# A linear-attention stage worked on pairs of chunks, two tokens to a partition, ahead of a convolution stage

## The chip, the cores and the metric

One core of a Trainium2 chip runs the whole kernel. The metric is device time in microseconds. Three runs of the kernel before took 157.04, 157.25 and 161.11 us, the median is 157.25. One further run was taken with the profiler; its time was 157.08 us, and the span that its trace covers is 155.3 us.

## What is computed

Two stages follow each other. The first is a linear attention with a decaying state: for each of 4 batches and 8 heads, 768 tokens, head size 48. The second is a gated circular convolution over the 768 tokens, in 384 channels (8 heads x 48), done with Fourier transforms. The reference, cut to what matters:

```python
for t in range(S):                                   # stage one, B=4, H=8, S=768, D=48
    cur = einsum('bhd,bhe->bhde', u[None] * kt, vt)
    y[:, :, t] = einsum('bhd,bhde->bhe', rt, state + cur)
    state = wt[:, :, :, None] * state + einsum('bhd,bhe->bhde', kt, vt)
x = y.transpose(0, 2, 1, 3).reshape(B, S, H * D)
proj = x @ w_proj                                    # stage two: three blocks of 384 columns
x1, x2, x3 = split(proj, 3)
x2_conv = irfft(rfft(x2, axis=1) * rfft(filter_fft, axis=0)[None], axis=1)
out = (x1 * x2_conv * x3) @ w_out
```

w lies between 0.8 and 0.95. All inputs and the output are float32.

## The kernel before

**Stage one, by chunks of 128 tokens.** 24 chunks (6 a batch) are worked one after the other. A chunk's 128 tokens lie in the 128 partitions. Loads go by groups: the first two groups hold one chunk each, all others two (`group`, line 1425). Each of w, k, r and v is loaded a chunk at a time, with runs of 48 numbers (192 bytes) in DRAM (line 1438); for the groups in `CASTS` v is loaded by POOL's queue instead and cast to bf16 on the way (line 1435). For each chunk i (`first`, line 1465):

- `ln`: ACT takes the log of w (line 1444); `cs`: PE sums the logs over the tokens with two triangular masks (lines 1473 and 1474, 384 columns each) and over the whole chunk with four matmuls of one column (line 1476); `ex`: ACT takes the exponential (line 1482); `kq`: DVE multiplies k and r by it (`scale`, shown at line 1328); `ph`: the chunk's whole decay (line 1493).
- `tr` and `qk`: k and q are turned by eight PE transposes (line 1501) and copied out of PSUM (line 1332 on ACT, 1334 on DVE); for the last chunks a DMA transpose on SP's queue does this instead (line 1507).
- `sc`: the scores of the 8 heads, eight matmuls of 48 x 128 x 128, two heads at a time in the upper and the lower half of the rows (line 1519). `mt` and `mc`: the mask, either as a product on DVE (line 1535) or as a copy on ACT and a cut on POOL by `affine_select` (line 1540).
- `kv`, `ki`, `su`: the state's update, eight matmuls of 64 columns (line 1560), the old state added with an identity (line 1566), and the decay on DVE (line 1570).
- `yi`, `ys`, `y`: the output y gathers in PSUM the term with u (`vc`, made by `rk`, `ru`, `rh`, `cc`, `vc` on POOL and DVE, added at line 1580, or later by DVE at line 1609), the term from the state (line 1589) and the masked scores times v (line 1597). `xn`, `yt`, `xT`: y is copied as bf16, turned (PE at line 1621, or DMA transpose at line 1630) and stored as xT.

**Stage two** (`second`, line 1761) for a batch: projections of xT (`p`, `q` at line 1768 and `xw` at line 1809), a sum and a difference of the two halves (`sd`, line 1820), the forward transform as matmuls with a table F (line 1655), products with the filter's spectrum (`u`, `p`, lines 1843 and 1846), the inverse transform (`E`, line 1865, with adds `aE` at 1903 and 1908 and `dE` at 1918), the gate (`yE`), the output projection (`o`, line 1950) and the store (line 1966). The tables F and mi are sines, made by ACT (line 1672) from angles that DVE and POOL compute; this needs another function table on ACT (`trig`, line 1666, and `table`, line 1716, back again).

**The order of the work** is written out by hand as the string `ORDER`: each line names an operation, the engine that does it ("-" for not at all), and, for what PE writes, the PSUM bank. Each engine works off its part in that order. `wproj`, `wout` and the casting loads of v stand in POOL's part, all other DMAs in SP's. A third word on POOL's lines ties it behind a named DVE instruction (line 1218). `warm n b` (line 1376) issues matmuls of zeros (line 1380) that no result needs. Stage two of a batch is interleaved with stage one of the next.

Of the kernel before, what the change touches and what calls it, by code (L numbers as in the profile page):

```python
# [20 lines left out]
L = 128  # L21
# [15 lines left out]
ADD, DVE2, ACT2, POOL2, FOLD, WIDE = "V", "M", "N", "C", "Q", "X"  # L37

NLW, NLD, NG, NF, NS, NX, NO = 3, 4, 3, 4, 3, 3, 4
CASTS = (2,4,6,8,10,12,)  # L40
NV, NVL = 6, 3
NTURN = 8
# [6 lines left out]
warm 16 4  # L49
first A  # L50
imaps G
smalls D
zeros D
pads D
signs D
lw0 S
lw3 S
kz1 D
ln0 A
maske G  # L60
lw2 S
lr0 S
u S
maskn G smalls
maps G
ang2 D
ia0.0 G
ia1.0 G
maski G
kz0 G pads  # L70
ang1 D
ang0 D
ia2.0 D
cs0 P 2
lk0 S
ln2 A
ex0 A
ew0 -
kq0 D
warm 8 0  # L80
warm 6 1
cs3 P 0
ex3 -
ia2.1 D
kw0 -
lw1 S
ur A
warm 4 5
um P 6
warm 5 5  # L90
tr0 P 4
lk3 S
lr3 S
ew3 X
lr1 S
lk1 S
kz2 G
ph0 A
ub A
ln1 A  # L100
lv0 S
rk0 G ang0
kz3 G kq0
ru0 G
rh0 D
cc0 D
qk0 A
kq3 -
kw3 G rh0
lv2 G cc0  # L110
warm 3 5
cs1 P 5
warm 3 7
sc0 P 3
mt0.1 D
mc0.1 -
lr2 S
lk2 S
vb0 G
vc0 G rh0  # L120
ex1 A
ph3 A
mt0.0 D
ew1 -
lv3 G
warm 3 7
cs2 P 0
warm 4 7
tr3 P 4
ex2 A  # L130
kq1 D
qk3 A
kw1 -
warm 2 7
tr1 P 7
mc0.0 -
rk1 D
ru1 D
rh1 G rk1
qk1 D  # L140
ph1 A
warm 3 2
sc3 P 4
kv0 P 2
su0 D
ew2 -
kq2 D
kw2 -
lv1 S
warm 2 3  # L150
sc1 P 6
yi0 P 2
y0 P
mt1.1 D
lw4 S
mt3.1 -
xn0 A
xa0 -
mt3.0 N
ph2 A  # L160
rk2 D
ru2 D
rh2 G rk2
vb1 A
tr2 P 3
warm 3 2
ki1 P 5
warm 2 2
kv1 P
lw5 S  # L170
lk4 S
lr4 S
qk2 A
ln3 A
mt1.0 D
cc1 D
yt0 P 2
lr5 S
lk5 S
lv5 S  # L180
warm 3 4
sc2 P 0
su1 D
warm 1 3
ki2 P 5
kv2 P
cc2 D
su2 D
cs4 P 6
ex4 A  # L190
wproj1 G
mc3.1 -
ki3 P 4
kv3 P
mt2.1 A
mc1.1 -
ia0.1 G
vc1 D
xT0 D
warm 2 3  # L200
yi1 P 2
ys1 P
vc2 G
mt2.0 D
mc1.0 -
y1 P
ew4 -
su3 D
mc2.1 G mt1.0
kq4 D  # L210
mc2.0 -
cs5 P 0
xn1 A
ex5 A
warm 1 4
yi2 P 3
ys2 P
y2 P
kw4 -
kq5 D  # L220
ew5 -
lw7 S
ph4 A
xn2 A
tr4 P 6
xa1 -
xa2 -
kw5 -
qk4 D
yt1 P 3  # L230
tr5 P 2
yi3 P 6
qk5 D
yt2 P 4
ph5 A
wproj0 G kq4
mc3.0 C
lv4 S
xT2 D
ys3 P  # L240
lr7 S
y3 P
xn3 D
sc4 P 4
mt4.0 D
xa3 -
trig A
sin2 A
rk3 G qk4
ru3 G qk5  # L250
warm 1 0
yt3 P 7
xT1 D
mt4.1 A
ia1.1 G mt4.0
warm 3 0
sc5 P 5
mt5.1 -
lw6 S
mt5.0 M  # L260
xw0.0 P 0
rh3 D
cc3 D
vb3 G rh3
sin1 A
vc3 G mt5.0
ki4 P 2
cxw0.0 D
xT3 A
warm 1 3  # L270
xw0.2 P 6
sin0 A
kv4 P
is A
cxw0.2 D
su4 D
warm 5 4
p0.2.0 P 5
p0.0.0 P 0
table A  # L280
lr6 S
lk6 S
lk7 S
mc4.1 G
filt S
lw8 S
lw9 S
cp0.0.0 D
yi4 P 6
yi5 P 2  # L290
ys5 P
lv7 G cxw0.2
mc5.0 -
mc5.1 -
ys4 P
y5 P
lk9 S
lk8 S
mc4.0 -
y4 P  # L300
xn4 D
if1 A
ln4 A
xn5 A
lv8 S
cs6 P 0
xa5 -
yt5 P 3
if0 A
ex6 A  # L310
lr9 S
xa4 -
yt4 P 2
xT5 D
xT4 D
cs7 P 6
ew6 -
kq6 D
ex7 A
ew7 -  # L320
xw0.4 P 2
lr8 S
kq7 D
ph6 A
cxw0.4 A
sd0.1.0 D
kw7 -
sd0.0.0 D
rk4 G
p0.2.1 P 4  # L330
cp0.2.1 A
ph7 A
kw6 -
lw10 S
p0.0.1 P 0
tr7 P 3
qk7 D
fsd0 D
fsd1 D
tr6 P 7  # L340
ru4 D
cp0.0.1 A
qk6 A
cp0.2.0 A
lv9 S
f0.2 P 0
cf0.2 A
sc6 P 6
mt6.1 -
mc6.1 -  # L350
mt6.0 N
f0.0 P 4
sc7 P 2
cf0.0 A
warm 2 0
h1 P 0
ln5 A
lv6 G sd0.1.0
h2 P 6
rh4 G fsd1  # L360
mt7.1 -
mt7.0 M
mc7.0 -
hc1 A
mc7.1 -
cc4 D
h0 P 2
hc2 A
kv6 P 4
hg1 D  # L370
hg2 D
hc0 A
cs8 P 0
su6 D
mc6.0 C
vc4 G
warm 2 5
yi6 P 6
y6 P
ex8 A  # L380
ew8 -
hg0 D
xn6 A
yi7 P 4
ys7 P
y7 P
xn7 A
xa7 -
xa6 -
cs9 P 6  # L390
kq8 D
yt6 P 3
ki7 P 2
kv7 P
su7 D
wproj2 G
yt7 P 4
xT7 D
ex9 A
xT6 A  # L400
kq9 D
kw8 -
rk5 G
ph8 A
ru5 D
rh5 D
cc5 D
ew9 -
tr8 P 5
ki8 P 2  # L410
qk8 A
ph9 A
vb5 G xT7
vc5 G
xw1.0 P 0
cxw1.0 A
kw9 -
tr9 P 3
qk9 A
kv8 P  # L420
sc8 P 4
su8 D
mt8.1 -
lw11 S
f0.1 P 0
ki9 P 6
kv9 P
mt8.0 M
if2 A
lk10 S  # L430
lk13 S
mc8.0 -
cf0.1 A
sc9 P 2
su9 D
q0.2.1 P 7
lr10 S
mt9.0 N
lk11 S
lr11 S  # L440
mt9.1 -
mc9.1 -
q0.0.1 P 5
lr13 S
yi9 P 0
q0.2.0 P 4
yi8 P 2
xq0.0.1 -
u10.0 D
lw12 S  # L450
ys9 P
ln6 A
ys8 P
cq0.0.1 D
lw13 S
mc8.1 -
y8 P
lv11 G su9
mc9.0 C
warm 5 2 192  # L460
y9 P
cs10 P 5
lr12 S
lv12 S
xq0.2.1 -
u00.0 D
xq0.2.0 -
xn8 A
xn9 A
q0.0.0 P 2  # L470
cq0.2.0 D
cq0.2.1 D
xq0.0.0 -
xa8 -
lk12 S
lv10 G
rk6 G
cq0.0.0 D
xa9 -
gq0.0.0 -  # L480
yt9 P 4
ex10 A
xT9 A
ru6 D
kq10 D
yt8 P 7
xT8 A
cs11 P 0
ex11 A
if3 A  # L490
kq11 D
warm 1 4
xw1.2 P 2
ew10 -
kw10 -
lk15 S
lv13 S
rh6 G ru6
cc6 D
ph10 A  # L500
lr15 S
gq0.2.0 -
lw15 S
lr14 S
p1.2.0 P 4
tr10 P 7
p1.0.0 P 5
cxw1.2 A
qk10 A
ew11 -  # L510
kw11 -
ph11 A
cp1.2.0 A
cp1.0.0 A
tr11 P 2
q1.0.0 P 0
# [1532 lines left out]
```

## Time and profile before

| | |
|---|---|
| profiled execution | 157.08 us, span 155.3 us |
| median of the runs shown | 157.25 us |
| PE, DVE, ACT, POOL busy | 142.3, 135.5, 117.5, 102.0 us |
| DMA packets, of them under 512 bytes | 112534, 108545 |
| moved | 27.12 MB, 175 GB/s over the span |
| share of the chain by engine | PE 65%, DVE 11%, DMA 9%, ACT 4%, SP's queue 4% |

How to read it: the span runs from the first to the last instruction of the profiled execution. A matmul's end is modelled, and matmuls overlap, so the price of one in a row of many is the distance of their starts. PE is the engine's matmuls, PEld its weight loads. In the rows of groups stand the line, the engine, the operation, out<-in, the count, then busy time in us and the mean of one in ns, then the idle time ahead of it and who ended it. Rows of stages give start:end, length, then busy time and count of each engine, the granted TensorE clock, the DMA share and GB/s. Rows of the chain give start, duration and the work. The line of DMA digits has 40 slices of 3.9 us.

### The profile page before, as it was taken

How to read it: one execution, taken by the hardware profiler on the slowest of the kernel's cores; microseconds unless marked ns; L12 is line 12 of the kernel's file. 1: busy time of each engine (PE TensorE's matmuls, PEld its weight loads, DVE VectorE, ACT ScalarE, POOL GpSimd, SP SyncE). 2: the span in 40 equal slices, each digit the busy share in tenths (PEclk: the TensorE clock that was granted, in tenths of full speed). 3: DMA queues.
4: the chain of work that ended last, by engine and by line, in shares of the span. 5: the costliest groups of instructions: out<-in, count | busy, mean ns of one | idle time of the engine just before them, and what ended most of it. 6: DMA issues, size and time to landing. Idle time of an engine off the chain costs nothing.

```text
span 155.3 us, 4220 instructions
## 1 busy us (share of the span) xinstructions
PE 142.3 (92%) x1634; PEld 89.4 (58%) x1634; DVE 135.5 (87%) x258; ACT 117.5 (76%) x195; POOL 102.0 (66%) x106
## 2 busy tenths in 40 slices
PE   7999894999999999999799999999999997999860
PEld 2455554656646767666566676665666664666430
DVE  4849984696999998999999999999999988799950
ACT  4584774897899894999879989989965575667650
POOL 6679595968229479589957988678796650802600
PEclk9999999699999999999999999999999999999997
DMA  5999999979999999899999918999997535000784
GB/s 105 227 212 218 194 145 215 200 135 339 177 187 213 198 181 180 142 199 176 187 192 201 179 25 144 220 193 189 178 183 149 155 122 209 0 0 34 294 330 159
DMA packets 112534, 27.12 MB, mean 175 GB/s; under 512 B 108545, under 2 KB 111106, under 8 KB 112514
## 3 DMA queue, kind: packets, MB, share of 16 engines
q1 hardware_dynamic: 98434, 24.49, 73.9%
q0 software_dynamic: 14080, 2.36, 20.0%
q8 instruction: 13, 0.21, 0.6%
q14 instruction: 7, 0.06, 0.1%
HBM read 22.41 MB, written 4.72 MB: 175 GB/s over the span
## 4 chain that ended last, share of the span: by engine, by line
PE 65%; DVE 11%; DMA 9%; ACT 4%; SPq 4%; issue 2%; DVEq 0%; ACTq 0%
PE banks L1768 13%; PE banks L1655 10%; PE banks L1380 7%; PE banks L1809 6%; PE banks L1950 5%; DMA kr<-in_k_dram 4%; PE banks L1865 4%; PE banks L1501 4%; SPq L1438 4%; PE banks L1519 4%; PE banks L1597 3%; DMA w<-in_w_dram 3%; DMA xT<-xn 3%; PE banks L1589 2%; PE banks L1473 2%
## 5 line engine op out<-in xcount | busy, mean ns | idle before, releaser
L1768 PE MATMUL banks<-xT,wproj 128*128 128x384 bf16 x144 | 27.3, 326 | 1.1 <-DVE xT L1334 1.0
L1328 DVE TENSOR_TENSOR kq<-banks,kr 128x768 bf16<-128x768 f32 x23 | 21.6, 950 | 3.1 <-DMA kr<-in_k_dram 2.7
L1328 POOL TENSOR_TENSOR vc<-vb,cc 128x768 bf16<-128x768 bf16 (+1 forms) x12 | 18.7, 1562 | 6.0 <-DVE sd L1820 3.1
L1328 POOL TENSOR_TENSOR rk<-kr 128x768 bf16<-128x768 f32 (+1 forms) x11 | 19.5, 1773 | 4.1 <-DMA kr<-in_k_dram 2.1
L1332 ACT ACTIVATE x<-banks 128x768 bf16<-128x768 f32 (+1 forms) x26 | 17.5, 687 | 5.2 <-PE banks L1809 3.0
L1482 ACT ACTIVATE banks<-banks 128x768 f32<-128x768 f32 x23 | 18.2, 798 | 1.9 <-PE banks L1476 1.6
L1535 DVE TENSOR_TENSOR mt<-banks,mask_excl 128x512 bf16<-128x512 f32 (+1 forms) x24 | 18.1, 772 | 1.3 <-PE banks L1519 1.1
L1768 PEld LDWEIGHTS <-wproj 128*128 128x128 bf16 x144 | 13.5, 98 | 9.3 <-issue 1.2
L1380 PE MATMUL banks<-wt 128*128 128x512 bf16 (+1 forms) x56 | 16.9, 397 | 1.1 <-DVE scl L1394 1.1
L1809 PE MATMUL banks<-wproj,xT 128*128 128x384 bf16 x72 | 13.7, 326 | 1.5 <-DMA xT<-xn 1.0
L1435 POOL DMA_DIRECT2D vb<-in_v_dram x12 | 11.3, 938 | 4.6 <-DVE sd L1820 3.3
L1540 POOL TENSOR_SCALAR_AFFINE_SELECT mt<-mt 128x512 bf16<-128x512 bf16 (+1 forms) x14 | 11.6, 834 | 3.5 <-ACT mt L1332 3.5
L1950 PE MATMUL banks<-wout,y 128*128 128x384 bf16 x72 | 13.3, 326 | 0.7 <-DVE y L1328 0.4
L1655 PE MATMUL banks<-sd,F 128*128 128x384 bf16 (+1 forms) x96 | 13.7, 328 | 0.0
L1501 PE MATMUL banks<-ident,kq 128*128 128x128 bf16 x144 | 11.1, 222 | 2.6 <-DVE kq L1328 2.1
L1332 ACT ACTIVATE qk<-banks 128x1024 bf16<-128x1024 bf16 x12 | 12.3, 1023 | 1.1 <-PE banks L1501 0.9
L1444 ACT ACTIVATE lg<-w 128x768 bf16<-128x768 f32 (+1 forms) x13 | 10.4, 798 | 3.2 <-DMA w<-in_w_dram 3.1
L1455 POOL TENSOR_TENSOR rk<-rk 128x384 bf16<-128x384 bf16 (+1 forms) x8 | 7.4, 921 | 7.7 <-DVE rk L1328 7.6
L1332 ACT ACTIVATE X<-banks 128x768 bf16<-128x768 f32 x12 | 9.8, 815 | 3.0 <-PE banks L1655 2.9
L1501 PEld LDWEIGHTS <-kq 128*128 128x128 bf16 x144 | 9.0, 98 | 4.9 <-DVE kq L1328 2.9
L1655 PEld LDWEIGHTS <-F 128*128 128x128 bf16 (+1 forms) x120 | 8.4, 103 | 5.6 <-issue 1.0
L1328 DVE TENSOR_TENSOR U<-X,hh 128x2304 bf16<-128x2304 bf16 (+1 forms) x12 | 11.6, 982 | 0.0
(118 smaller groups left out, 338.3 us busy)
## 6 DMA issues: line engine op xcount, KB each, us to landing
w<-in_w_dram SPq DMA_DIRECT2D x24, 192.0 KB, 4.2
kr<-in_r_dram SPq DMA_DIRECT2D x24, 192.0 KB, 4.5
kr<-in_k_dram SPq DMA_DIRECT2D x24, 192.0 KB, 4.5
out_dram<-o SPq DMA_DIRECT2D x9, 384.0 KB, 2.9
v<-in_v_dram SPq DMA_DIRECT2D x12, 192.0 KB, 4.0
vb<-in_v_dram POOLq DMA_DIRECT2D x12, 96.0 KB, 5.5
U<-in_moe_filter_fft_dram SPq DMA_DIRECT2D x1, 1152.0 KB, 6.0
wproj<-in_moe_w_proj_dram POOLq DMA_DIRECT2D x3, 288.0 KB, 5.1
```

Source lines behind the costliest of these rows:

```text
L1328: return eng(e).tensor_mul(o, a, b)
L1332: return nc.scalar.activation(out=o, in_=a, func=AF.Copy)
L1380: nc.tensor.matmul(banks[:, at, lo:hi], wt[:, 0:L], x, start=True, stop=True)
L1435: op(f"lv{i}", [POOL], lambda e, bk, q=q, rw=rw: nc.gpsimd.dma_start(out=vb[fv][:, q], in_=v[b, :, rw, :].rearrange("h t d -> t h d")), w= ...
L1482: return nc.scalar.activation(out=o, in_=x, func=AF.Exp)
L1501: nc.tensor.transpose(p[:, HP * m + j, :], kq[f][:, m, 2 * j:2 * j + 2, :], ident)
L1535: return copy(ACT, o, x) if e in (ACT, ACT2) else nc.vector.tensor_mul(o, x, _mid(mask_excl, z - HP * a))
L1540: return nc.gpsimd.affine_select(out=o, in_=o, pattern=[[0, z - HP * a], [1, L]], compare_op=ALU.is_gt, fill=0.0, base=0, channel_multipli ...
L1655: nc.tensor.matmul(p[rows], F[:, ti, c0 + rows.start:c0 + rows.stop], x[q][:, ti, :], start=(ti == 0), stop=(ti == NT - 1),)
L1768: nc.tensor.matmul(p, wproj[:, cb, col0:col0 + L], xT[bx][:, cb, sl], start=(cb == 0), stop=(cb == CB - 1),)
L1809: nc.tensor.matmul(view(bk)[:, z], xT[bx][:, cb, (c0 + z) * L:(c0 + z + 1) * L], wproj[:, cb, C:2 * C], start=(cb == 0), stop=(cb == CB - 1),)
L1950: nc.tensor.matmul(view(bk)[:, z], yt_[:, z, :], wout[:, cb, :], start=(cb == 0), stop=(cb == CB - 1),)
```

## The change

- A group is a pair of chunks, 256 tokens, from the first on; there are 12. k, r and v are loaded by pairs: the lower 64 partitions hold the first chunk, the upper 64 the second, and each partition two neighbouring tokens j = 0 and 1, which makes runs of 96 numbers (384 bytes). w is loaded by chunks as before. One group casts v by POOL's DMA queue; otherwise v goes through SP's queue and is cast by POOL or ACT.
- All work on keys goes by a "slot" j: 64 tokens of each of both chunks. `cs` is made of matmuls with 64 columns, one for each chunk; scores, `kv`, and `yx` (the state's term for the half of the heads that lie in the other half of the rows) use a quarter of the array, 64 or 48 rows by 64 columns; `yi`, `ys` and `y` use half of the rows. The whole decay of both chunks is summed with the first slot.
- The order of tokens inside a pair follows into xT: the angles of the sines, the filter's load (now two DMAs) and the output projection (two halves of 64 columns where two blocks are stored together) are adapted.
- Masks: a matrix `later`, made by `affine_select`, is DVE's factor; POOL's cut works on the two partition halves one after the other. 10 whole and 8 half masks are copied by ACT, 6 whole and 8 half ones are DVE products.
- The halving `rh` may be left out, with `cc` summing over 48 instead of 24 numbers: this is so in 7 of the 12 pairs. The term `vc` is always added on PE.
- Options of the old operations are gone: `xn` as an add on DVE, `xa` and the products `kw` on POOL.
- ORDER is new. The sines stand behind the exponentials of the first pair; 28 matmuls of zeros stand ahead of the second pair, none later. 10 of the 24 slots are turned by DMA transposes (two each), and 13 chunks of xn. The inverse transform is folded on PE for three of the four batches (`E` with Q; before for two and a third of one).

Counts by engine, as the two programs list them: matmuls 1634 before, 2496 after; POOL's cuts 14 and 36; SP's input loads 84 and 59 (the filter and u left out); DMA transposes 11 and 33.

The diff's core (`across` is `yx`, `yy` is `y`; the part with `dma_start_transpose` turns a slot on SP's queue):

```diff
-    kr = tiles(NLD, [L, 2, 2, H, D], FP32, "kr")
-    vl = tiles(NVL, [L, 2, H, D], FP32, "v")
+    kr = tiles(NLD, [L, 2, H, 2, D], FP32, "kr")
+    vl = tiles(NVL, [L, H, 2, D], FP32, "v")
...
+        def pair(x):
+            return x[b, :, rows, :].rearrange("h (p j) d -> p h j d", j=2)
...
+            op(f"l{name}{gi}", [SP], lambda e, bk, m=m, t=t: nc.sync.dma_start(out=kr[sl][:, m], in_=pair(t)),
...
-            nc.tensor.matmul(p[:, 0, 0:C], mask_neg, lgq[:, :, 0:D], start=True, stop=True)
-            nc.tensor.matmul(p[:, 1, 0:C], mask_excl, lgq[:, :, 0:D], start=True, stop=True)
-            for j in range(HP):
-                nc.tensor.matmul(p[:, 1, C + j:C + j + 1], lgq[:, 2 * j:2 * j + 2, :], ones, start=True, stop=True)
+            for a, m in enumerate((mask_neg, mask_excl)):
+                for x in (0, 1):
+                    nc.tensor.matmul(p[part[x], a, 0:C], m[:, j, :], lg[fg][:, x, :, 0:D], start=True, stop=True)
+            if j == 0:
+                for x in (0, 1):
+                    for h in range(H):
+                        c = C + HP * x + h // 2
+                        nc.tensor.matmul(p[part[h % 2], 1, c:c + 1], lg[fg][:, x, h, :], ones, start=True, stop=True)
...
+            for a in range(HP):
+                for par in (0, 1):
+                    p0 = DP * par
+                    for x in (0, 1):
+                        nc.tensor.matmul(
+                            p[part[x], par, a, :], turned(bk, p0, 0, x, a, j), both(bk, p0, x, a),
+                            start=True, stop=True)
...
+            def cut(e, bk):
+                z = a + 1 if e == POOL else 2
+                for x in (0, 1):
+                    o = mt[s_][part[x], HP * a:HP * z, :]
+                    got = nc.gpsimd.affine_select(
+                        out=o, in_=o, compare_op=ALU.is_gt, fill=0.0, base=-j, channel_multiplier=-2,
+                        pattern=[[0, HP * (z - a)], [1, 2], [2, DP]])
...
+            for j in (0, 1):
+                for h in range(H):
+                    for x in (0,) if final else (0, 1):
+                        nc.tensor.matmul(
+                            kvp(bk, x)[part[h % 2], h // 2, :], kq[fk[j]][part[x], 0, h, :], vb[fv][part[x], h, j, :],
...
+        def across(e, bk):
+            for a in range(HP):
+                for j in (0, 1):
+                    for x in (0, 1):
+                        p0 = DP * (1 - x)
+                        nc.tensor.matmul(
+                            yat(bk, x)[part[j], 2 * a + 1 - x, :], turned(bk, p0, 1, x, a, j),
+                            state(x)[p0:p0 + D, a, :], start=(a == 0), stop=False)
...
+        def yi(e, bk):
+            for j in (0, 1):
+                for par in (0, 1):
+                    for x in (0, 1):
+                        c, hs = DP * (1 - j + x), slice(par, H, 2)
+                        nc.tensor.matmul(yat(bk, x)[:, hs], wide[part[x], c:c + L], vc[fg][part[x], hs, j, :],
+                                         start=False, stop=False)
+        def ys(e, bk):
+            for a in range(HP):
+                for x in (0, 1):
+                    p0 = DP * x
+                    o, s_ = yat(bk, x)[:, 2 * a + x, :], state(x)[p0:p0 + D, a, :]
+                    nc.tensor.matmul(o, both(bk, p0, x, a), s_, start=False, stop=False)
+        def yy(e, bk):
+            for j in (0, 1):
+                for h in range(H):
+                    for x in (0, 1):
+                        nc.tensor.matmul(
+                            yat(bk, x)[:, h, :], mt[fs[j]][part[x], HP * (h % 2) + h // 2, :], vb[fv][part[x], h, j, :],
+                            start=False, stop=(j == 1 and h == H - 1))
...
+                if e == SP:
+                    for x in (0, 1):
+                        nc.sync.dma_start_transpose(
+                            out=qk[gi % NQ].rearrange("p (b x) (j t) -> p b x j t", x=2, j=2)[:, :, x, j],
+                            in_=kq[f][part[x]].rearrange("p a h d -> p (a h d)"))
...
-                            nc.tensor.matmul(
-                                view(bk)[:, z], yt_[:, z, :], wout[:, cb, :],
+                            for x in range(n):
+                                o, lo = (view(bk)[:, z], 0) if n == 1 else (view(bk)[DP * x:DP * x + DP, z], L * x + DP * z)
+                                nc.tensor.matmul(
+                                    o, yt_[:, lo:lo + L // n], wout[:, cb, :], start=(cb == 0), stop=(cb == CB - 1))
```

The start of the new ORDER, PE's, ACT's and SP's part of it: SP loads `lw1 lw0 lk0 lr0 lr1 lv0 lk1 lw3 lw5 lw2 lw4 lk2 lr2`; ACT does `ln0.0 ln0.1 ub ex0 ex1 ph0 trig is sin2 sin0 sin1 table ln1 ln2 ex3`; PE does `warm 14, um, warm 10, cs0, cs1, warm 14, tr1, tr0, warm 6, sc1, sc0, kv0, warm 6, ki1, warm 6, cs3`.

2361 lines of the change are left out of this document (1087 added, 1274 removed).

## Prediction

> **What bounds the kernel now.** I read the page's totals first, then busy time by stage, then the chain of work that ended last, then the timeline of one stretch for the price of each kind of matmul.
>
> ```profile
> span 155.3 us, 4220 instructions
> PE 142.3 (92%) x1634; PEld 89.4 (58%) x1634; DVE 135.5 (87%) x258; ACT 117.5 (76%) x195; POOL 102.0 (66%) x106
> DMA  5999999979999999899999918999997535000784
> q1 hardware_dynamic: 98434, 24.49, 73.9%
> ```
>
> PE, DVE and, until slice 29 (about 112 us), the DMA engines are all near full. Part of PE's time is filler, the zero matmuls of line 1380. The two fences below have the busy time by stage (length, then PE, PEld, DVE, ACT, POOL), first of all instructions, then of line 1380 alone (PE, PEld):
>
> ```profile
> 0.00:20.00 20.00, 17.98 (x166) 9.38 (x167) 15.16 (x52) 12.80 (x21) 14.73 (x33) 1.00 1.13 192
> 20.00:40.00 20.00, 17.48 (x219) 11.43 (x219) 14.71 (x25) 14.84 (x23) 15.03 (x14) 0.91 1.08 207
> 40.00:115.00 75.00, 73.43 (x950) 48.78 (x948) 72.77 (x113) 66.82 (x116) 56.72 (x47) 1.00 1.11 176
> 115.00:150.00 35.00, 33.26 (x303) 19.85 (x301) 32.25 (x69) 22.45 (x37) 15.55 (x13) 1.00 0.48 136
> ```
>
> ```profile
> 0.00:20.00 20.00, 11.99 (x38) 3.45 (x38) 1.00 1.13 192
> 20.00:40.00 20.00, 2.79 (x9) 0.86 (x9) 0.91 1.08 207
> 40.00:115.00 75.00, 2.13 (x9) 0.79 (x9) 1.00 1.11 176
> ```
>
> PE's real work is therefore 6.0 us of the first 20, 14.7 of the next 20, 71.3 of 75, 33.3 of 35. After 40 us PE is the bound and DVE (72.8 of 75) stands just behind it. Before 40 us it is the input: the chain waits there for a load of k, and the first chunks' work goes in step with it.
>
> ```profile
> 18.69 6.65 DMA kr<-in_k_dram
> 25.46 0.97 DVE kq L1328
> ...
> 54.31 0.33 PE banks L1519 x8
> 54.64 1.10 PE banks L1655 x12
> ...
> 82.84 0.24 PE banks L1560 x8
> ...
> 97.31 0.45 PE banks L1501 x8
> 97.83 0.36 PE banks L1560 x16
> ...
> 116.37 0.97 PE banks L1655 x6
> ...
> 119.44 0.20 PE banks L1589 x8
> ...
> 124.83 0.31 PE banks L1589 x16
> ```
>
> So the change is worth what it takes from PE after 40 us, as far as DVE follows, and what it takes from the wait before.
>
> **PE, step by step.** Small matmuls go in packs when they use different parts of the array: line 1589 (48 rows) takes 0.20 us for 8 and 0.31 for 16, so a pair of row halves costs 0.026 us and the block 0.10 beside. Line 1560 (64 columns): 0.36 less 0.24 over four pairs, 0.030 a pair, 0.12 beside. Line 1655 at 384 columns in column halves: 12 in 1.10, against 6 whole ones in 0.97, so 0.162 a pair and again 0.12 beside. That fixed part, about 0.107, falls due where one shape of tile follows another. The rest is in the timeline (start, duration):
>
> ```profile
> 67.37 0.62 PE L1519 MATMUL banks<-qk 48*128 48x128 bf16 x16
> 67.92 0.31 PE L1560 MATMUL banks<-vb,kq 128*64 128x48 bf16 x8
> ...
> 69.09 0.33 PE L1580 MATMUL banks<-vc,ident 128*128 128x192 bf16 x2
> 69.35 0.27 PE L1589 MATMUL banks<-S,qk 48*128 48x48 bf16 x8
> ```
>
> From start to start: scores 16 in 0.55 (with line 1519's 8 in 0.33, 0.056 a pair), the vc matmul (0.26 less 0.107) / 2, about 0.08. A transpose is 0.45 / 8 = 0.056.
>
> The changed program's own list gives the counts. Sums of logs (cs): 48 whole matmuls become 96 column halves, 48 pairs at 0.162: 0. Its one-column matmuls: 96 at 0.026 become 96 pairs at 0.030: +0.3. Transposes of kq, 144 to 112: -1.8; of xn, 57 to 33: -1.3; they go to SP's DMA transposes. Scores: 96 row pairs become 96 packs of four (row half times column half): 0 if four run as two do. State (kv): 80 column pairs become 80 packs of four: 0. vc into y (yi): 32 become 48 row pairs: 16 x 0.08 = +1.3. State into y: 80 row pairs become 48 packs of four (yx) and 48 row pairs (ys): +0.6. y: 192 become 192 row pairs: 0. Inverse transform, fewer whole ones by the folded form: -0.6. Output projection in column halves: 0. Changes of tile shape: I count 108 in the list before, 95 after: -1.4. Sum -2.9.
>
> No row shows four tiles at once. The bounds are 0 (a pack of four costs what a pair does) and twice that: scores +5.4, kv +2.4, yx +1.4, so -2.9 to +6.3 in all. I take the low end: rows and columns each halve without loss in the rows above, and the four matmuls touch four different parts. The Trainium skill (TensorEngine Tiling (Array Packing), Key properties) says that different tiles load weights and multiply in parallel and that changing the tiling mode drains the array, which agrees with the 0.10 to 0.12 us of the blocks above. The same skill (TensorE: Matmul & The Clock Gate, the section on 56 ns) puts a floor of 25 ns under every start-to-start; by it the 860 further matmuls would add some 21 us; line 1589's 16 in 0.31 us are 19 ns each with the drain, so the rows speak against it for packs of two, and for four it is rival E.
>
> **DVE, ACT, POOL.** Prices:
>
> ```profile
> L1535 DVE TENSOR_TENSOR mt<-banks,mask_excl 128x512 bf16<-128x512 f32 x20 | 13.2, 682 | 0.4 <-PE banks L1519 0.4
> L1535 DVE TENSOR_TENSOR mt<-banks,mask_excl 128x1024 bf16<-128x1024 f32 x4 | 4.9, 1221 | 0.9 <-PE banks L1519 0.7
> L1908 DVE TENSOR_TENSOR y<-ev,banks 128x384 bf16<-128x384 f32 x9 | 4.9, 546 | 0.6 <-ACT ev L1332 0.6
> L1328 POOL TENSOR_TENSOR vc<-vb,cc 128x768 bf16<-128x768 bf16 x11 | 17.9, 1629 | 6.0 <-DVE sd L1820 3.1 <-DVE cc L1458 2.0 <-ACT vb L1332 0.8
> L1540 POOL TENSOR_SCALAR_AFFINE_SELECT mt<-mt 128x1024 bf16<-128x1024 bf16 x6 | 6.6, 1096 | 2.7 <-ACT mt L1332 2.7
> L1540 POOL TENSOR_SCALAR_AFFINE_SELECT mt<-mt 128x512 bf16<-128x512 bf16 x8 | 5.1, 638 | 0.8 <-ACT mt L1332 0.8
> ```
>
> DVE loses 12 half masks and gains 2 whole (-5.7), loses 8 adds of vc to y and 8 behind the inverse transform (16 at 0.55, -8.8), the spectrum's seven copies (of the same length, -4) and 8 shorter turns of xT (-2); it takes 5 vc and 4 more rk products, 3 more with u, and 7 sums over 48 instead of 24 (+13 if they cost what DVE rows of their length do), and some copies (+4). That leaves about -3, with -6 and +1 as bounds: DVE goes down as far as PE and stays just behind it. ACT gets four more whole masks, xn in pairs and the spectrum's copies, loses four qk copies: about +6, on an engine with 8 us free between 40 and 115. POOL's cuts work on half the partitions, so each mask needs two: 14 become 36. At the rows' prices that is 20 x 1.1 + 16 x 0.64 = 32 instead of 12; five vc products, four rk, the v casts by DMA and most halvings of rk leave: POOL's sum stays about 98.
>
> **Loads and the start.** A packet's price from two windows of the DMA queue (100 to 112 us, then 130 to 150: packets, MB, share of 16 engines):
>
> ```profile
> q1 hardware_dynamic: 11128, 2.23, 98.8%
> ```
>
> ```profile
> q1 hardware_dynamic: 883, 2.42, 31.0%
> ```
>
> 200 bytes take 12 x 16 x 0.988 / 11128 = 17 ns, 2741 bytes 112 ns. A packet of 384 bytes lies between 17 ns and twice that; on the line between the rows, 24. The inputs of a pair were 8 x 1024 packets of 200 bytes, 8.7 us; now they are 2 x 1024 such (w) and 3 x 1024 of 384: 5.4 to 8.7, 6.8 by the line. The loads of v with a cast on POOL's queue go from twelve to one. The DMA transposes go from 11 to 33, 20 of them of half a kq; SP issues them in order ahead of loads; its input loads go from 84 to 59, so the 22 further transposes cost SP nothing as long as one takes no longer to issue than a load, and up to their excess where a load stands behind. So the wait of 20 to 40 us goes: PE's loss there, 20 - 14.7 = 5.3, should fall to the 5% of the next stage, 1 us: about -4. Against it, all work goes by whole pairs: the first kq still has four loads ahead of it, but the w of pair 1 comes eleventh in SP's queue, at about 16 us, until when PE has one pair to work on, and the second stage waits for whole pairs too. I put +2 for that, between 0 and the 4 won. The sines and two table loads (6.6 us of ACT) sit behind the first pair's exponentials; the logs of pair 1 wait behind them, but for the w of 16 us anyway, so they cost nothing while that cover holds, and up to 6.6 if w came at once.
>
> Sum: 155.3 - 2.9 (PE) - 4 + 2 (start) = 150.4 us of span; the end behind the last projection is unchanged. The profiled run took 157.08, 1.8 beside its span, and the median shown is 157.25, so about 152.
>
> **Rivals.**
> A, slower: packs of four cost two pairs. Place: scores, kv, yx. Speaking for it: no row shows four; against: both halvings are free. The Trainium skill (the Tiling page, Restrictions) says that column tiling switches fast weight load off; line 1560's 0.030 against 0.026 is all that shows here. +9.2 over the forecast: 161. It is slower than before by over 2% once a pack of four costs 1.9 pairs.
> B, slower: POOL becomes the bound. The cut's pattern has one more step than line 1540's and a half-partition form that no row shows; at twice the price POOL has 130 us of work, which must be done before the last 30 us: about 163. It decides from about 1.5 times.
> C, no change: the start is not shorter, because pairs are twice as coarse: the 4 us stay lost and the 2 are added: 156.
> D: packets of 384 bytes cost 34 ns and loads are no faster: the same 156, so part of C.
> E, slower: in quarter tiles nothing overlaps: 384 scores at 0.056 instead of 96 packs (+16), 320 kv and 192 yx at 0.030 instead of 128 packs (+12): about 180. Both halvings in the rows speak against it.
>
> **Chances.** Forecast 0.50, A 0.14, B 0.10, C and D 0.21, E 0.02, a larger gain (148, if the start gives its whole 4 and DVE loses 6) 0.03. Two percent, about what a measurement of this kernel can tell, is 154.1 and 160.4: faster 0.53, same 0.21, slower 0.26. The range takes in C, A and the low end of the start: 146.5 to 162; the forecast's own is 149 to 154.5.
>
> **What would show it.** Right: 16 scores in about 0.33 us and 32 kv matmuls in about 0.34; PE's real work over 40 to 115 us at 95% or more with no filler; POOL cuts at 1.1 us; the first kq near 9 us and no load waited for after 20. Wrong: score blocks of 0.5 us (A), y waiting for POOL's cuts (B), PE half idle or at half clock between 12 and 30 us (C).

## The result and the profile after

The changed kernel took 172.94 us (median of 4 runs, 172.88 to 174.89) where the kernel before took 158.48 (157.04 to 161.11): a ratio of 1.104, 95% interval 1.090 to 1.117. It is slower; the forecast was 152.0 with 146.5 to 162. The profiled execution took 172.88 us, its span is 171.2. Ratios below are against the kernel before on the same chip; they leave disturbed runs out, so that they can differ a little from the ratio of two medians.

From the page of the changed kernel:

```profile
span 171.2 us, 5906 instructions
PE 140.2 (82%) x2496; PEld 92.2 (54%) x2496; DVE 143.7 (84%) x238; ACT 122.3 (71%) x183; POOL 102.8 (60%) x109
PEclk9999985895799999999999999999999969999999
q1 hardware_dynamic: 80354, 28.29, 73.5%
q8 instruction: 19, 0.31, 0.8%
```

PE is busy 2.1 us less than before and idle 31.0 us of its span instead of 13.0. DVE has 8.2 us more work. Where PE is idle, by stages (the columns as in the prediction), with the last of these stages in the kernel before behind it, and then the three stretches in which the clock was at half:

```profile
20.00:40.00 20.00, 10.86 (x307) 8.56 (x308) 10.04 (x14) 9.35 (x17) 14.77 (x16) 0.77 1.02 225
...
96.00:136.00 40.00, 30.10 (x632) 20.12 (x626) 36.04 (x45) 26.32 (x38) 29.09 (x21) 1.00 0.79 148
```

```profile
96.00:136.00 40.00, 38.83 (x462) 24.56 (x460) 37.90 (x65) 30.34 (x52) 27.11 (x23) 1.00 0.82 159
```

```profile
24.03:30.86 6.83, 4.10 (x115) 3.23 (x117) 3.00 (x4) 5.74 (x10) 4.70 (x4) 0.50 1.06 271
37.68:44.51 6.83, 5.60 (x92) 4.73 (x93) 3.58 (x4) 2.98 (x4) 0.91 (x2) 0.50 0.95 179
136.67:140.08 3.41, 3.41 (x26) 1.92 (x24) 3.38 (x3) 2.29 (x4) 2.92 (x2) 0.50 0.74 77
```

Two stretches lose: 20 to 40 us (PE 9.1 us idle, before 2.5) and 96 to 136 us (9.9 us idle, before 1.2; DVE is busy 36.0 of 40). In the half-clock stretches PE was busy for 13.1 us with work that would take half of that, 6.6 us, at full clock (an estimate from the granted clock of 0.50).

A sum over all of PE's rows, each matmul counted until the next starts, closes the account. Before: real work 127.5, filler 14.8, idle 6.7, ahead of the first and behind the last matmul 6.2. After: 130.8, 9.4, 25.2, 5.8. At full clock the real work is 126.2 before and 124.2 after. So of the 15.9 us of span: real work -2.0, half clock +5.3, filler -5.4, idle +18.5, ends -0.4.

The chain of the changed kernel names the idle parts. In the start:

```profile
16.93 7.15 DMA w<-in_w_dram
...
24.23 0.69 issue
24.91 0.79 ACT banks L1315
...
25.80 0.92 ACT qk L1133
...
26.76 0.64 PE banks L1368 x16
...
33.84 0.24 PE banks L1417 x15
34.08 4.83 issue
38.91 0.20 PE banks L1417
```

A load of w for the fourth pair (it lands at 24.08 us) holds ACT, whose queue has the log of that pair ahead of the copy of a turned slot (`qk` of slot 3); the scores of the second pair start 3.8 us late. At 34.08 PE stops for 4.83 us between two matmuls of one block, and nothing releases it ("issue"). Later:

```profile
98.42 3.93 DVE U L1129 x2
102.36 0.02 issue
102.38 2.19 DVE P L1723
...
108.85 4.08 DMA xT<-xn
...
115.69 0.87 SPq L1500
116.56 0.05 issue
116.61 3.93 DMA xT<-xn
...
129.32 1.42 DVE y L1129
130.74 2.46 DVE y L1795 x2
```

Here the chain goes through DVE instructions and through two turns of xn by SP's DMA transposes (`xT<-xn`). The DVE rows are longer than in the kernel before. Groups by form, first before, then after:

```profile
L1328 DVE TENSOR_TENSOR kq<-banks,kr 128x768 bf16<-128x768 f32 x23 | 21.6, 950 | 3.1 <-DMA kr<-in_k_dram 2.7 <-ACT banks L1482 0.2
L1328 DVE TENSOR_TENSOR U<-X,hh 128x2304 bf16<-128x2304 bf16 x6 | 8.5, 1412 | 0.0
L1328 DVE TENSOR_TENSOR y<-y,g 128x768 bf16<-128x768 bf16 x8 | 4.5, 598 | 0.0
L1918 DVE TENSOR_TENSOR y<-y 128x384 bf16<-128x384 bf16 x6 | 1.9, 351 | 0.0
```

```profile
L1129 DVE TENSOR_TENSOR kq<-banks,kr 128x768 bf16<-128x768 f32 x24 | 22.2, 948 | 5.6 <-ACT banks L1315 5.6
L1129 DVE TENSOR_TENSOR U<-X,hh 128x2304 bf16<-128x2304 bf16 x6 | 10.2, 1738 | 0.0
L1129 DVE TENSOR_TENSOR y<-y,g 128x768 bf16<-128x768 bf16 x7 | 7.7, 1111 | 0.0
L1795 DVE TENSOR_TENSOR y<-y 128x384 bf16<-128x384 bf16 x10 | 5.2, 541 | 0.0
L1388 POOL TENSOR_SCALAR_AFFINE_SELECT mt<-mt 64x1024 bf16<-64x1024 bf16 x20 | 31.1, 1554 | 8.3 <-ACT mt L1133 7.5
L1388 POOL TENSOR_SCALAR_AFFINE_SELECT mt<-mt 64x512 bf16<-64x512 bf16 x16 | 12.0, 749 | 9.6 <-ACT mt L1133 8.6 <-PE banks L1468 0.4
```

kq, which reads one operand from PSUM, is as long as before (948 and 950). U, y times g and y, which read two operands from SBUF, are longer in the mean by a quarter to nearly twice; the cuts, 1554 and 749 ns, stand above the 1096 and 638 of the whole ones before. One by one, a y times g takes 547 ns alone and 1504 beside a cut, a cut of 1024 columns 1155 at its shortest and 2285 beside such products. Over all DVE instructions, the time above the shortest of each form is 16.0 us after and 5.0 before. That is the 11 us by which DVE's sum missed the forecast (-3 forecast, +8.2 found). Of the 16.0 us, 13.8 lie in instructions that ran mostly beside a cut; of the 5.0 before, 0.2.

### The profile page after: what moved, and what is told of

Its sections match the earlier page's. It is cut to its first block, busy times and chain, and to the rows that moved or that the text cites. A ratio compares the mean times of both kernels' runs of the same rounds, so it can differ in the third digit from the quotient of the medians.

```text
span 171.2 us, 5906 instructions
## 1 busy us (share of the span) xinstructions
PE 140.2 (82%) x2496; PEld 92.2 (54%) x2496; DVE 143.7 (84%) x238; ACT 122.3 (71%) x183; POOL 102.8 (60%) x109
## 4 chain that ended last, share of the span: by engine, by line
PE 39%; DVE 25%; DMA 9%; issue 6%; POOL 4%; ACT 4%; SPq 1%; ACTq 0%; DVEq 0%; POOLq 0%
PE banks L1645 8%; PE banks L1829 6%; DVE kq L1129 5%; PE banks L1526 5%; DMA xT<-xn 5%; DMA w<-in_w_dram 4%; PE banks L1686 4%; DVE U L1129 4%; PE banks L1368 3%; PE banks L1742 3%; DVE rk L1129 2%; DVE y L1129 2%; PE banks L1331 2%; DVE P L1723 2%; DVE g L1671 2%
## 5 line engine op out<-in xcount | busy, mean ns | idle before, releaser
L1388 POOL TENSOR_SCALAR_AFFINE_SELECT mt<-mt 64x1024 bf16<-64x1024 bf16 (+1 forms) x36 | 43.1, 1196 | 17.9 <-ACT mt L1133 16.1
L1129 POOL TENSOR_TENSOR rk<-kr 128x768 bf16<-128x768 f32 x7 | 12.7, 1814 | 8.9 <-DMA kr<-in_r_dram 7.4
L1133 ACT ACTIVATE mt<-banks 128x1024 bf16<-128x1024 f32 (+1 forms) x18 | 14.6, 832 | 4.7 <-PE banks L1368 4.4
L1368 PE MATMUL banks<-qk 48*64 48x128 bf16 x384 | 10.0, 235 | 7.7 <-ACT qk L1133 3.8
L1829 PE MATMUL banks<-wout,y 128*64 128x384 bf16 (+1 forms) x138 | 14.5, 359 | 0.0
L1129 POOL TENSOR_TENSOR vc<-vb,cc 128x768 bf16<-128x768 bf16 x7 | 10.3, 1474 | 5.9 <-DVE cc L1279 4.4
L1526 PE MATMUL banks<-sd,F 128*128 128x384 bf16 (+1 forms) x96 | 13.2, 327 | 0.8 <-DVE kq L1129 0.8
L1382 DVE TENSOR_TENSOR mt<-banks,later 128x512 bf16<-128x512 f32 (+1 forms) x14 | 12.6, 910 | 1.5 <-PE banks L1368 1.0
L1129 DVE TENSOR_TENSOR U<-X,hh 128x2304 bf16<-128x2304 bf16 (+1 forms) x12 | 13.1, 1144 | 0.0
L1671 DVE TENSOR_TENSOR g<-banks,x 128x768 bf16<-128x768 f32 (+1 forms) x12 | 9.8, 816 | 3.4 <-PE banks L1645 3.4
L1368 PEld LDWEIGHTS <-qk 48*64 48x64 bf16 x384 | 7.0, 115 | 10.2 <-issue 4.7
L1133 ACT ACTIVATE xn<-banks 128x768 bf16<-128x768 f32 (+1 forms) x13 | 9.8, 763 | 2.2 <-PE banks L1468 2.1
```

The source lines that it names most:

```text
L1129: return eng(e).tensor_mul(o, a, b)
L1133: return nc.scalar.activation(out=o, in_=a, func=AF.Copy)
L1368: nc.tensor.matmul(p[part[x], par, a, :], turned(bk, p0, 0, x, a, j), both(bk, p0, x, a), start=True, stop=True,)
L1382: return copy(ACT, o, x_) if e in (ACT, ACT2) else nc.vector.tensor_mul(o, x_, _mid(lat, HP * (z - a)))
L1388: got = nc.gpsimd.affine_select(out=o, in_=o, compare_op=ALU.is_gt, fill=0.0, base=-j, channel_multiplier=-2, pattern=[[0, HP * (z - a)], ...
L1526: nc.tensor.matmul(p[rows], F[:, ti, c0 + rows.start:c0 + rows.stop], x[q][:, ti, :], start=(ti == 0), stop=(ti == NT - 1),)
```

## The experiments

The theories. P (neighbours): POOL's cuts stretch DVE's SBUF work, and are stretched by it, on the path. S (start): the order of loads and of ACT's queue. F: PE's instructions come late. C: missing filler lets the clock fall. T: turns of xn on SP's queue. Each was a rival to the others. Lines of ORDER in the diffs have the operation, its engine (S for SP, P for PE, G for POOL, A for ACT, D for DVE, - for not at all) and the bank; lines between are left out at "...". In what follows a slot is also called a chunk. The runs come from several chips, on which the kernel before took 158.4 to 159.3 us in the median, so differences of less than 1 us between experiments mean nothing.

**E1: the cuts left out.** The causal mask of the scores that ACT copies is then missing from the result, here and in E8 and E14.

```diff
-                    for x in (0, 1):
-                        o = mt[s_][part[x], HP * a:HP * z, :]
-                        got = nc.gpsimd.affine_select(...)
-                    return got
+                    return None
```

> The changed kernel without POOL's 36 cuts; the causal masking of the scores that ACT copies is left out. Theory P (neighbour): while a cut runs on POOL, DVE's instructions from and to SBUF last up to three times as long; in the changed kernel DVE's rows stand 16.0 us above their shortest forms (5.0 before), and those stretches lie on the chain at 98 to 104 and 126 to 133 us. By it DVE's sum falls from 143.7 to about 133, y times g from 1111 to about 600 ns, the PE gaps of 102.5 and 132.4 us close, and the time falls by 6 to 10 us to 163 to 167. Rival S (the loss lies in the first 45 us: late w, PE's instructions, half clock): DVE's sum may fall, but the time only by 0 to 2 us, 171 to 173.

Ratio 1.052 (1.036 to 1.068), median 168.25 us (165.65 to 170.6). The ratio goes by the two lowest runs, 165.65 and 167.69 us, 6.3 us less than the changed kernel in the middle: the low end of what P said. In the traced run, of 170.6 us, DVE's sum fell to 130.6 (129.9 in E8, 130.5 in E14), POOL's to 60.6, the excess over the shortest forms to 3.6 us; the waits of 102.5 and 132.4 us are gone. DVE came as P said.

**E2: the log of the fourth pair later on ACT.**

```diff
-ln3 A
 ...
 ex4 A
 ...
 ph2 A
+ln3 A
```

> The logs of the fourth pair are moved on ACT behind the first phi of the third pair, so that the exponentials of chunk 4 and the turn of chunk 3 no longer stand behind a w that lands at 24 us. Theory S: the PE gap of 3.8 us at 22.9 us shrinks below 1 us and the half clock that follows it (24 to 31 us) goes; time 168 to 170. Rival: the gap is only moved, because PE meets its next wait (instructions, k of the next pair) just as late: time 172 to 173.5.

Ratio 1.068 (1.058 to 1.077), 169.42 us: 3.5 us less than the changed kernel. The wait of 3.8 us is gone; the next one, 2.3 us for v at 25 us, came in its place, and no pause stood at the place of 34 us. The half clock of 24 us did not go, which S had expected; it moved to 27.4 to 37.7 us. In time S is right for this step.

**E3: the filter's load later.**

```diff
-filt S
 ...
 lr4 S
+filt S
```

(and `fsd0`, `fsd1` behind `cc3`.)

> The load of the filter (1.2 MB) is issued after r of the fifth pair instead of at 26 us, and the two sums on it stand later on DVE. Theory F (instructions): PE's pause of 4.8 us in the middle of a kv block at 34 us, which nothing releases, is a 16 KB packet of instructions that stands behind the loads in full rings; with less to load then it comes earlier and the pause falls below 1.5 us, and the half clock of 37.7 to 44.5 us with it: time 166 to 170. Rival: PE has simply run through its instructions, which come at their own pace: the pause stays at 4 to 5 us, somewhere in the same 200 instructions, and the time within 1.5 us.

Ratio 1.118 (1.100 to 1.136), 178.0 us. PE's pause fell to 1.1 us, as F said, but DVE then waited for the filter and PE 4.3 us for DVE at 44.7 us, and the clock was at half from 22 to 42 us. As a price of the pause the run tells nothing.

**E4: turns of pairs 7 and 8 on PE.**

```diff
-yt7 - 2
-xT7 S
+yt7 P 2
+xT7 A
-yt8 - 1
-xT8 S
+yt8 P 3
+xT8 A
```

> The turns of xn of pairs 7 and 8 go back from SP's DMA transposes to PE, with ACT copies. Theory T: SP issues them in order behind loads and turns of kq, so that PE waits 2.8 us at 117.8 and 0.65 us at 112.3; both waits go, PE gains 0.7 us of work: time down by 2 to 3 us, 170 to 171. Rival: DVE is the bound in that stretch (its next waits are kq's) and the 3 us come back there: time within 1 us of 172.9.

Ratio 1.085 (1.077 to 1.092), 171.86 us. The first projection of the third batch stood ahead of the turn here and worked on older values, so E7 repeats it in better places.

**E5: E2 and the order of loads.**

```diff
+lv1 S
 lw6 S
 ...
 lw7 S
-lv1 S
 ...
-wproj0 G
 ...
-wproj1 G
 ...
 vb1 G
+wproj0 G
+wproj1 G
```

> E2's edit, and the order of the loads: v of the second pair is issued ahead of w of the fourth, and the first two thirds of the projection's weights (0.6 MB) behind the second cast of v on POOL instead of at 14 us. Theory S: PE's wait of 2.3 us at 25 us in E2 is for that v, behind loads that are not needed yet; it falls below 0.7 us, and PE's real work done by 40 us rises by 2 us or more; time 1.5 to 3 us below E2's 169.4, 166.5 to 168. Rival: the rings are full until 45 us whatever the order, so that another load is late by as much: time within 1 us of E2.

Ratio 1.066 (1.057 to 1.075), as E2: the rival. One run, the profiled one, took 433.6 us, so no trace of E5 is used; the other three took 168.3 to 170.2 us, the middle one 168.67.

**E6: E5 with more filler.** `warm 14 0` became 20, `warm 6 4` became 8 in a bank of its own, `warm 6 7` twice became 10 and 16.

> E5 with 22 more half fillers (54 instead of 32 of 512 columns after rounding, 256 columns each) in PE's waits between 11 and 17 us. Theory C (clock): the half clock between 24 and 45 us comes from PE's idle time in the 10 us ahead of it; with those waits filled it shrinks to 3.4 us or goes, and the time falls by 2 to 4 us. Rival: PE waits for loads there, and what the clock takes it has as idle time anyway: the clock may rise, the time stays within 1 us of E5.

Ratio 1.068 (1.062 to 1.075): no gain. PE's idle time before 20 us, behind the first matmul, fell to 1.6 us (3.8 in the changed kernel), yet the clock was at half from 27.5 to 41.2 us, longer than in E2. C fell: the time is the rival's.

**E7: E5 with the turns of pairs 7 and 8 on PE.** As E4, with `yt7 P 6` behind `y8` and `xT8 A` ahead of `cxw2.2`.

> E5 with the turns of xn of pairs 7 and 8 on PE and ACT, in places where the projections still come behind them. Theory T: the PE waits for DMA-turned xT near 109 and 115 us (3.6 us together in E2) go, for 0.7 us of work: 2 to 3 us below E5. Rival: the next waits there are DVE's (kq) and take them back: within 1 us of E5.

Ratio 1.049 (1.040 to 1.057), 166.60 us: 2.1 us below the 168.67 of E5, the intervals just apart. The waits for xT are gone, though 1.8 us for kq stand in their place. T holds, at the low end of what it said.

**E8: E5 without the cuts.** The edit of E1.

> E5 without POOL's cuts; the causal masking of the scores that ACT copies is left out. Theory P: the cuts' cost (E1: DVE 130.6 instead of 143.7 us, time 5 us less) and the start's add up, because they lie in different stretches (96 to 135 us and before 45): 5 to 6 us below E5, about 161 to 162. Rival: the two are one, PE and DVE being bound by each other: 2 us or less below E5.

Ratio 1.034 (1.026 to 1.042), 163.99 us: 4.7 us below the 168.67 of E5. The cuts and the start add up, nearly as expected.

**E9: E7 with w of the second pair first.**

```diff
 lr0 S
+lw3 S
+lw2 S
-lr1 S
 ...
 lk1 S
+lr1 S
 ...
-lw3 S
 lw5 S
-lw2 S
```

> E7, with w of the second pair issued right behind the first pair's w, k and r, and r of the second pair behind its k. The prediction's price for coarser pairs: PE has one pair until w of the second lands at 16 us. If that is what holds the start, the logs of the second pair start by 13 us or as soon as ACT's sines are done, PE's wait of 1.2 us before the second pair's sums goes, and the time falls by 1 to 2 us below E7. Rival (the sines): ACT works on sines and table loads until about 16 us whatever lands, so nothing moves: within 0.7 us of E7.

Ratio 1.054 (1.046 to 1.061), 166.58 us as E7: the rival, the sines. The load was issued at 3.9 us instead of 8.0 and the log still started at 16.1, as ACT's rows of E9 show:

```profile
9.39 1.28 ACT L1539 ACT_TABLE_LOAD   x1
...
12.23 2.57 ACT L1545 ACTIVATE F<-o,mpi 128x768 bf16<-128x768 uint16 x3
14.82 1.28 ACT L1589 ACT_TABLE_LOAD   x1
16.11 0.84 ACT L1264 ACTIVATE lg<-w 128x768 bf16<-128x768 f32 x1
```

**E10: the sines behind the second pair.** E9, with `trig`, `is`, `sin2`, `sin0`, `sin1`, `table` moved behind `ex2`, and `ln1` behind `ph0`.

> E9, with the sines and their two table loads moved on ACT behind the exponentials of the second pair. By the prediction's step the sines cost up to 6.6 us once w comes early: then this edit brings the second pair's first kq from 19.6 us to 16 or earlier and the time 2 us or more below E9. Rival: the 6.6 us of ACT only stand in front of the third pair instead, or the half clock takes the gain: within 1 us of E9.

169.25 to 172.32 us, the two lowest (169.25 and 169.34) 2.7 us above E9; there is no ratio. The second pair's first kq was done at 19.4 instead of 19.9 us, and PE then waited 5.4 us for the third pair's, whose exponentials stood behind the sines. So the sines stand in front of the third pair, as the rival said, and cost more there than it said.

**E11: six chunks masked by DVE.** E7, with `mt8.0`, `mt9.0`, `mt10.0`, `mt14.0`, `mt16.0`, `mt17.0` as "M" and their cuts as "-".

> E7, with six chunks (8, 9, 10, 14, 16, 17) masked by DVE on its way out of PSUM (1.22 us each) instead of copied by ACT and cut by POOL, those whose cuts run beside DVE's work on SBUF at 86 to 140 us. Theory P: DVE pays 6 x 1.22 = 7.3 less 0.7 (a half that it masked already) and wins back the 7 to 9 us by which the cuts lengthen it there, y no longer waits for cuts: DVE's sum changes by less than 3 us, time 1 to 3 us below E7. Rival (the cuts only fill POOL, DVE is bound by its count of instructions): DVE's sum goes up by 6 to 7 us and the time by 2 to 5.

Ratio 1.074 (1.066 to 1.081), 170.12 us: 3.5 us above E7. DVE's sum stayed (144.4 and 143.9), its excess fell only from 16.1 to 11.4: the cuts beside DVE at 120 to 136 us are those of chunks 18 to 21, which the edit leaves in place. PE waited 2.5 us for a mask that stood behind U and P on DVE. In time the rival is right.

**E12: filler between the packs.** E7, with `warm 4 1` behind `sc3` and `y0` and `warm 6 1` behind `sc2`.

> E7 with 14 halves of filler (1.5 us at full clock) between the packs of small tiles of the second and third pair, at 22 to 27 us. Theory C2: the clock is halved there because small tiles keep little of the array busy, and PE waits there anyway (vc, instructions); with filler between them the half clock (28.5 to 38.8 us) shortens by 3.4 us or more, the pause for instructions shrinks, and the time falls by 1 to 3 us. Rival: the filler only stands in the way: time up by 0 to 2 us.

Ratio 1.063 (1.056 to 1.071), 168.16 us: 1.5 us above E7, the intervals overlapping slightly. The half clock there did shorten by 3.4 us, as C2 said (32.3 to 39.1 us, 28.5 to 38.8 in E7), but PE's pause grew from 1.3 to 3.3 us and the time did not fall. C2 fell in time.

**E13: E9 with one kq ahead on DVE.**

```diff
-dE1.2.1 D
 ...
 ex23 A
+kq23 D
+dE1.2.1 D
 ...
-kq23 D
```

> E9, with the kq of chunk 23 moved on DVE ahead of two y differences and a y times g, which the cuts lengthen from 1.2 to 3.9 us together. Theory P with its place on the path: PE's wait of 3.15 us at 126 to 132 us, and the half clock behind it, is DVE's queue standing in front of that kq; it falls below 1 us, the time by 2 to 4 us below E9's 166.6: 163 to 164.5. Rival: what waits behind (the output projection of batch 1, whose y is now later) takes it back: within 1 us of E9.

Ratio 1.058 (1.048 to 1.067), as E9. The wait of 3.15 us went, and 1.0 us at 128 and 3.2 us at 133 us, both for DVE, came back. One place in the queue is worth nothing here, as the rival said: DVE is busy for 22.8 of the 24 us from 112 to 136 us.

**E14: E13 without the cuts.** The edit of E1.

> E13 without POOL's cuts; the causal masking of the scores that ACT copies is left out. If the start's waits, the turns, the place of kq and the cuts are all there is, this comes to the time of the kernel before or just above it: 158 to 161. If it stays above 163, a large part of the loss is somewhere else.

Ratio 1.010 (1.000 to 1.020), 160.09 us: 8 us below E13. From its groups:

```profile
L1129 DVE TENSOR_TENSOR y<-y,g 128x768 bf16<-128x768 bf16 x7 | 3.8, 548 | 0.0
```

These instructions are as short as they are alone (U takes 1416 ns, before 1412). So with the start's and the turns' edits and no cuts, the loss against the kernel before is accounted for to within 2%; the gain that was forecast is not, for 152 lies 8 us lower. The kernel before has 14 cuts itself; without them it was not run.

**E15: the kernel before with half-partition cuts.**

```diff
-                return nc.gpsimd.affine_select(out=o, in_=o, ..., base=0, channel_multiplier=-1)
+                for x in (0, 1):
+                    o = mt[s2_][64 * x:64 * x + 64, HP * a:z, :]
+                    got = nc.gpsimd.affine_select(out=o, in_=o, ..., base=-64 * x, channel_multiplier=-1)
+                return got
```

> The kernel before, with each of its 14 cuts made by two instructions over 64 partitions each, as the changed kernel makes them; nothing else. The price alone: a cut over 64 partitions takes 0.64 to 0.70 us for 512 and 1.1 to 1.25 for 1024 columns, so that POOL's sum goes from 102 to 113 to 116. Theory P: DVE's instructions beside them are stretched by 2 to 5 us in all and the time goes up by 1 to 3 us. Rival: POOL has room and DVE is not touched: the time stays within 0.7 us of 158.5.

Ratio 1.044 (1.034 to 1.054), 165.77 us against 159.27: 6.5 us from this alone, where P had said 1 to 3. Its groups of cuts and its waits:

```profile
L1541 POOL TENSOR_SCALAR_AFFINE_SELECT mt<-mt 64x1024 bf16<-64x1024 bf16 x12 | 14.7, 1221 | 1.5 <-ACT mt L1332 1.0
L1541 POOL TENSOR_SCALAR_AFFINE_SELECT mt<-mt 64x512 bf16<-64x512 bf16 x16 | 10.4, 648 | 1.0 <-ACT mt L1332 0.4
```

```profile
PEld L1599 <- POOL mt L1541: 3.0, 4, 1.6
PE banks L1599 <- POOL mt L1541: 2.3, 3, 1.3
```

Half the partitions cost as much as all (1096 and 638 in the kernel before). The price was as forecast; what it does was not: DVE's sum went from 135.5 to 141.0 and y waited for cuts, on an engine, POOL, that is busy 70% of the span. DVE's excess rose from 5.0 to 9.9 us, and only half of the rise lies in instructions that ran mostly beside cuts; the rest ran beside POOL's other work.

**E16, E17, E18: the kernel before with less filler.** E16 leaves out the 18 matmuls of zeros behind 20 us, E17 the 36 behind 9 us, E18 all 56.

> The kernel before without the 18 filler matmuls behind the first 20 us (the changed kernel has none there); nothing else. Theory C: with waits of 1 to 2 us left open the clock is halved for 3.4 us or more at further places: granted clock below 0.96, time up by 1 to 4 us. Rival: the filler fills only waits, and the clock holds without it: within 0.7 us of 158.5.

> The kernel before with its first 20 filler matmuls (up to 9 us) and none of the 36 behind them; E16 kept 38, up to 20 us. Theory N (filler stands in the way where PE's waits end sooner than the filler): as fast as E16 or up to 1.5 us faster, 154.5 to 156, with the clock at half once for 3.4 to 7 us. Theory C (filler holds the clock): without it between 9 and 20 us the clock is at half for 7 us or more between 12 and 30 us and the time 2 us or more above E16.

> The kernel before with no filler matmul at all. Theory C: the first sums and turns run at half clock from the start and PE never fills a window before 25 us: 2 to 5 us above E16, 157.5 to 161. Theory N: PE waits for loads there at either clock: within 1.5 us of E16.

E16: 155.72 us, ratio 0.980 (0.973 to 0.987); the clock is at half for 6.8 us instead of 3.4, and neither expectation had the gain. E17: 156.98 (152.69 to 157.11), too uneven for a ratio; it decides nothing. E18: 155.65, ratio 0.980 (0.973 to 0.987), as N said. So the kernel before without its filler beats both kernels; whether by 2%, the interval leaves open. In E18 the clock is at half until 29 us. The granted clock in its rows does not show that, having no entry before then; PE's rows do, where three transposes take 0.53 us and, from 29 us on, 0.33. Eight transposes of kq take 0.83 us from start to start at 27.03 and at 28.18 us, 0.45 in the kernel before.

```profile
27.86 0.53 PE L1594 MATMUL banks<-ident,xn 128*128 128x128 bf16 x3
...
29.18 0.33 PE L1594 MATMUL banks<-ident,xn 128*128 128x128 bf16 x3
```

No filler and half clock in the whole start together cost this kernel nothing against E16, which has filler there: 155.65 and 155.72 us. That it waits for its inputs at either clock is the likely reason.

## Why the prediction failed, step by step

**PE, right.** Real work at full clock -2.0 us against -2.9 forecast. Packs of four cost as a pair. Timeline of the changed kernel:

```profile
84.44 0.44 PE L1417 MATMUL banks<-vb,kq 64*64 64x48 bf16 x32
84.71 0.62 PE L1368 MATMUL banks<-qk 48*64 48x128 bf16 x32
85.27 0.50 PE L1686 MATMUL banks<-wproj,xT 128*128 128x384 bf16 x2
```

From start to start 32 kv matmuls take 0.27 us and two blocks of 16 scores 0.56, so 0.28 a block where 0.33 was forecast. Rivals A and E are out. What did not hold is that this gain comes off the span: PE's share of the chain fell from 65% to 39%, DVE's rose from 11% to 25%. The Trainium skill's floor of 25 ns (TensorE: Matmul & The Clock Gate, the section on 56 ns) does not hold for these, which lie in different tiles: 0.27 us / 32 is 8 ns.

**Packets of 384 bytes, right.** One window of the queue (60 to 63 us, nearly all of them 384 bytes long):

```profile
q1 hardware_dynamic: 2134, 0.80, 98.3%
```

3 x 16 x 0.983 / 2134 = 22 ns, where the line between two rows gave 24. Rival D is out. The first kq came at 8.5 us, near the 9 forecast.

**"So the wait of 20 to 40 us goes: -4", wrong.** This is the first step that failed. PE was idle for 9.1 us of these 20; the forecast was 1. Faster packets do not help what stands in a queue behind an instruction that waits: the log of pair four on ACT (E2: 3.5 us, the largest single term found in the start). Neither v sooner (E5) nor w sooner (E9) gave anything more. The +2 for pairs was about right as far as the first 20 us show: filler and idle behind the first matmul make 13.2 us instead of 11.7. "They cost nothing while that cover holds", of the sines, stands: with w early the log starts no sooner (E9), and put elsewhere they cost more (E10). Rival C (the start not shorter) was the nearest to what happened in the start, at 156, but it put the loss on coarse pairs.

**"DVE about -3, POOL about 98", wrong.** The second failure, and the largest. The cut's price by itself was right (1.16 and 0.66 us at the shortest), the count too, and without the excess DVE's sum would have fallen by 2.8 us; but the prices were added as if the engines did not know of each other. Rival B looked for it in POOL's sum, which is not the bound (60%); E8 and E14 show that leaving the cuts out is worth 4.7 and 8 us, E15 that making them in halves costs 6.5 us in the other kernel. The row that could have told stood in the trace of before: one halving of rk on DVE took 2017 ns beside POOL's products, and 350 otherwise. A rule of the Trainium skill that the prediction did not use says the same: GpSimd and VectorE share SBUF interfaces, with contention for DVE instructions that have two SBUF inputs (GPSIMD Engine Reference, Specifications). The forms agree: y times g (two from SBUF) goes from 547 to 1504 ns, kq (one from PSUM) stays at 948. How much of the cuts' price is DVE's stretching and how much is y waiting for POOL, the runs do not separate; that the waits of y alone (1.2 us at 96 to 136 us) are small in the changed kernel speaks for the former there, those of E15 for the latter.

**"22 further DMA transposes cost SP nothing", wrong** in two places: a turn of xn is issued in order behind turns of kq that wait for DVE, and then takes 3.9 to 4.1 us to land. E7: 2.1 us.

**Filler**, which the prediction did not price: it took filler as something that only fills waits. E16 and E18 show that what is left out can be a gain. The half clock of the changed kernel (+5.3 us of PE time) lies mostly behind the start's waits, and filler did not buy time back there (E6, E12); what it costs by itself was not shown.

Together: 150.4 us were forecast for the span, 171.2 were found. The start's net gain of 2 became a loss of 3.5 (E2), the turns cost 2.1 (E7), the cuts 4.7 to 8 (E8, E14). With all of these edits E14 takes back 13 of the 21 us; the other 8 stay open. Candidates are PE's idle time in the start beyond E2, the half clock, and PE's pause for instructions, of which E3 does not tell the price, as it brought another wait.

## What to carry over

The sums of two engines are not independent: before instructions are added to POOL, look which DVE instructions with two SBUF operands will run beside them, and take the lengths from rows with such a neighbour. A faster transfer is worth what the waiting engine's queue has next, so read what stands behind each waiting instruction, not how full the rings are. And leave out the filler once: a matmul of zeros may cost time, as it did in the kernel before (E16, E18).

## What was not expected of the hardware

PE's pause comes at one and the same place. In the changed kernel PE stops behind its 479th matmul, in the middle of a block, for 4.83 us. Its variants stop there too, for 0.6 (E11) to 4.4 us (E1); E2 does not. In E6 and E12, which have filler ahead, it is the same number and not the same matmul. Where E6 pauses a second time it is behind the 351st, and E11 and E14 behind the 607th: 128 away. Timelines of the changed kernel and of E7:

```profile
33.67 0.41 PE L1417 MATMUL banks<-vb,kq 64*64 64x48 bf16 x15
38.91 0.20 PE L1417 MATMUL banks<-vb,kq 64*64 64x48 bf16 x1 [4.83 <-issue]
```

```profile
31.80 0.62 PE L1417 MATMUL banks<-vb,kq 64*64 64x48 bf16 x15
33.68 0.20 PE L1417 MATMUL banks<-vb,kq 64*64 64x48 bf16 x1 [1.27 <-issue]
```

The queue of instruction packets has 19 packets for 2 x 2496 matmuls and weight loads, and 13 for 2 x 1634 before: about 256 instructions, or 128 matmuls, to a packet of 16 KB. In the changed kernel the third packet was under way from 36.31 to 37.45 us, and PE went on at 38.91. In all 13 traces with the pause PE goes on 1.4 to 1.8 us after the third packet has landed, and in E2 that packet landed 2.9 us ahead of the place. So the pause ends when that packet is there. PE had passed its 351st matmul at 31.54: a packet's worth was used up in 2.5 us, while packets of loads kept the DMA engines busy. In the kernel before 128 matmuls last 8.9 us or more up to there, and it does not pause so. That the packet is late because it stands behind the loads is argued from these times, and E3 (less to load, pause of 1.1 us) agrees; it wasn't tried alone.

Each stretch at half clock that ends inside a span lasts 3.41 us or a multiple (6.83, 10.24, 13.65 and more in these traces). How busy PE was in such a window does not tell when the clock comes back: in E2, windows in which PE was busy 98% and 87% left it at half and one of 100% brought it back, but in E1 and E8 windows of 85 to 87% brought it back, and in E3 two of 100% did not.
